# Attention and gated MLP on one core: block 0's transposes behind two QKV tiles, the projection of blocks 2 and 3 a chunk later, two ties more

## The chip, the cores and the metric

The kernel runs on one core of a Trainium2 chip. The metric is device time in microseconds (us), from start to end of one execution; lower is better. The profile is of one execution. Its engines are PE (TensorE, matmul), PEld (PE's weight loads), DVE (VectorE), ACT (ScalarE), POOL (GpSimd) and SP (SyncE, which here only issues DMAs). Each works through its own instructions in order and waits for the others by semaphores.

## The reference

One layer for 2048 tokens of width 576, in float32. First attention with 32 heads of 18 channels, in which a token sees itself and seven earlier ones at distances 2, 4, ... 14; then a gated MLP of hidden width 4608. Both add to their input, and both are preceded by a layer norm without weights.

```python
h  = x + attn(layernorm(x) @ wqkv) @ wo
g  = layernorm(h) @ w_gate
u  = layernorm(h) @ w_up
h2 = h + (sigmoid(g) * u) @ w_down
```

## The kernel before

**Blocks.** Since attention only joins tokens of equal parity, the tokens are four blocks of 512: even ones, first and second half (blocks 0 and 1), and odd ones likewise (blocks 2 and 3). A block is four tiles of 128 tokens (NS = 4).

**Precision.** Every float32 operand is split in a high and a low part by `split` (lines 103 to 105: ACT copies the high part, line 104, DVE subtracts it, line 105; `split_rest`, lines 108 and 109, for the last 64 of 576 rows). A product is three matmuls: high by high, low by high, high by low. The transposes that come before are matmuls with the identity (`tr_main`, line 139, and `tr_rest`, line 143).

**Front.** `qkv` (line 377) computes the QKV projection of a block for a quarter of the heads, one token tile of 14 matmuls (`tok_major`, lines 146 to 153) at a step, copies it out on ACT (line 384) and sends it to DRAM. `attention` (line 162) is DVE work on windows that are loaded back: products (182, 208), sums (186, 214, 216, 219) and the softmax between (194 to 200, Exp on ACT). `step(ag, n)` moves it on by n steps; so QKV tiles are put between its steps. Block 0's result is kept in `o` (a `tok` tile, line 409 completes it), that of the other blocks goes to DRAM (lines 221 and 223).

**Block 0's projection.** `front` (line 478) transposes `o`, multiplies it by the output weights, adds the input (line 255), normalises (`ln_j`, lines 113 to 135) and transposes again for the MLP. In before (lines 502 to 521) two of its steps, the transposes, come right behind block 0's attention, tied with `issue_after(last)` behind the last QKV tile emitted; its other steps stand between the QKV tiles of blocks 2 and 3 for the last quarter of heads. `issue_after(x)` keeps an instruction behind x in the order of x's engine.

**Main loop** (line 1078). It goes over 86 chunks c: 14 of kind "std" for block 0 (`single`, line 623), 22 of kind "pair" for blocks 0 and 1, 14 "std" for block 1, 36 "pair" for blocks 2 and 3. NF is 36 and NSTD 14. A chunk is 128 of the 4608 hidden channels: gate and up products (`prod`, line 588, and `rest`, line 595), a Sigmoid on ACT, a product on DVE. "Pair" handles two blocks with seven products in place of eight (`pair`, line 649), whose operands and results are sums. Its copies, sums and Sigmoids have lines 654 to 678. `load_gu` (line 544) loads the next weights `wg` on SP; `weights` (line 554) splits them. Down products (`down_tile`, line 697) are copied or added to a `stage` tile (lines 705 and 707), and POOL's DMA of line 713 adds a full one to `hacc` in DRAM.

**Background work.** At fixed places in a chunk `bg_step` takes one step of a generator: `under_first` for block 1, `under_rest` (line 882) for blocks 2 and 3: attention, then `proj_scr` (line 792) of each. `proj_scr` loads the attention output `oj` (one tile per three steps), the weights `wow` and the input `hj`, all by `load_j` and `paced` (line 549), tied behind the last weight load on SP (`behind`); transposes, multiplies and normalises them. `wos_early` (line 779) loads half of the output weights into two `tl` tiles. In `under_rest` the projection of block 2 may begin from chunk NF on (line 893). Between the blocks, line 901 clears a `stage` tile on POOL, from which ACT writes zeros to DRAM (line 903).

**Last 36 chunks.** Here the down products of blocks 2 and 3 are in sevens too (`down_seven`, line 748: matmuls 759, copies 765). Their weights `wd` come in a load of their own (`load_down`, line 972) for two chunks at a time; `down_side` (line 982) forms sums of them on DVE (lines 1003 to 1006) and splits them into `d` tiles (`pair_d`) at steps 0, 4 and 6 of an odd chunk. The seven products are queued behind `lag(LAG)`, three empty steps, in the first case (f == 1).

**Results.** Near the end of each block's accumulation in `hacc`, line 1083 copies `hacc[0]` and `hacc[1]` to the output from POOL.

The order within an engine is made by a scheduler from the order of emission and the priorities (`tc.high_priority`).

## Time and profile before

| | |
|---|---|
| median of three runs | 1597.37 us (1594.46 to 1597.83) |
| the profiled execution | 1599.5 us, of which the span from first to last instruction 1597.7 |
| mean granted PE clock | 0.996 |
| busy: PE, DVE, ACT, POOL | 1561.7, 1268.7, 874.0, 185.4 us |
| DMA | 273.50 MB, mean 171 GB/s |

In the views below a group or wait is named by engine, line and `out<-in` tiles. In a list of waits, "PE acc L143 <- DVE tok L409: 4.5, 1, 4.5" says that PE's instruction of line 143 writing `acc` stood for DVE's instruction of line 409, 4.5 us in all, once, at most 4.5. In a timeline a row has the start, the duration, engine, line, operation and tiles, "xN" for N instructions in a run, and in brackets the idle time before it and what ended it. In a chain of waits a row is start, duration and what the end of the program then hung on. PE clock is the share of full speed that was granted.

### The profile page before, as it was taken

The numbers are of one execution on the slowest core, as the hardware profiler recorded it, in microseconds if no ns is written. First come the engines' busy times: TensorE is split into PE (matmuls) and PEld (weight loads), VectorE is DVE, ScalarE is ACT, GpSimd is POOL, SyncE is SP. The second block draws the span as 40 slices with busy tenths as digits, with TensorE's granted clock in tenths as the row PEclk, the third lists the DMA queues.
The fourth block names the chain that finished last, engine by engine and source line by source line (L and its number), as shares of the span: only waits on it lengthen the run. The fifth ranks groups of instructions, "written<-read, shape, count | busy, mean of one in ns | idle before, by whom it ended". The sixth has DMA issues, their size and how long they took to land.

```text
span 1597.7 us, 22339 instructions
## 1 busy us (share of the span) xinstructions
PE 1561.7 (98%) x8532; PEld 1381.1 (86%) x8532; DVE 1268.7 (79%) x1922; ACT 874.0 (55%) x1535; POOL 185.4 (12%) x226
## 2 busy tenths in 40 slices
PE   7999899999999999999999999999999999999998
PEld 6899888898888888888898887888888888888887
DVE  7999999769999999999355777776677776677755
ACT  5432235334556555656434444766777676677761
POOL 1000010010000100000120100112112111211110
PEclk9999999999999999999999999999999999999999
DMA  7564545534566676666864225889888989888983
GB/s 268 200 210 161 193 183 195 200 115 174 133 169 163 165 178 172 166 181 146 239 207 152 84 94 141 164 172 177 169 170 188 176 166 183 172 167 179 187 171 119
DMA packets 76699, 273.50 MB, mean 171 GB/s; under 512 B 8272, under 2 KB 14160, under 8 KB 75696
## 3 DMA queue, kind: packets, MB, share of 16 engines
q0 software_dynamic: 27856, 106.47, 35.3%
q1 hardware_dynamic: 40304, 143.70, 27.4%
q10 hardware_dynamic: 8432, 21.89, 3.6%
q8 instruction: 67, 1.10, 0.3%
q14 instruction: 40, 0.33, 0.1%
HBM read 145.88 MB, written 128.52 MB: 172 GB/s over the span
## 4 chain that ended last, share of the span: by engine, by line
PE 83%; DVE 9%; DMA 5%; issue 2%; ACT 1%; SPq 0%; POOL 0%; ACTq 0%; POOLq 0%; DVEq 0%
PE b L588 41%; PE dp L697 13%; PE dp L759 11%; PE b L595 7%; PE acc L150 6%; DMA wg<-in_wmlp_dram 1%; PE b L150 1%; DVE pr L208 1%; PE bgp L150 1%; DVE tl L105 1%; DMA x<-tok 1%; DVE w L105 1%; DMA ar<-x 1%; DMA oj<-o 1%; DVE stage L707 1%
## 5 line engine op out<-in xcount | busy, mean ns | idle before, releaser
L588 PE MATMUL b<-tl,w 128*128 128x512 f32 x1728 | 443.2, 396 | 2.5 <-ACT w L104 2.2
L588 PEld LDWEIGHTS b<-tl,w 128*128 128x128 f32 x1728 | 312.0, 188 | 63.1 <-ACT w L104 3.0
L588 PE MATMUL b<-th,w 128*128 128x512 f32 x1380 | 360.2, 395 | 3.0 <-ACT s L671 1.7
L588 PEld LDWEIGHTS b<-th,w 128*128 128x128 f32 x1380 | 251.1, 188 | 57.1 <-DVE s L672 5.5
L595 PE MATMUL b<-th,w 128*128 128x512 f32 x576 | 177.7, 390 | 0.0
L104 ACT ACTIVATE w<-wg 128x384 fp32r<-128x384 f32 (+2 forms) x200 | 118.2, 596 | 103.2 <-PE b L595 40.5
L765 ACT ACTIVATE ev<-dp 128x576 f32<-128x576 f32 x224 | 145.1, 648 | 33.8 <-PE dp L759 31.0
L105 DVE TENSOR_TENSOR w<-wg,w 128x384 fp32r<-128x384 f32 (+2 forms) x200 | 128.3, 648 | 43.9 <-ACT w L104 43.6
L768 POOL DMA_DIRECT2D h<-ev x128 | 109.4, 855 | 457.1 <-ACT ev L765 445.0
L150 PE MATMUL acc<-qw,th 128*128 128x432 f32 x512 | 155.9, 365 | 1.0 <-DVE th L109 0.9
L105 DVE TENSOR_TENSOR w<-tw,w 128x512 fp32r<-128x512 f32 x116 | 79.6, 687 | 72.4 <-ACT w L104 71.4
L595 PEld LDWEIGHTS b<-th,w 128*128 128x128 f32 x576 | 108.4, 188 | 23.3
L104 ACT ACTIVATE w<-tw 128x512 fp32r<-128x512 f32 x116 | 73.2, 631 | 92.3 <-PE b L588 83.2
L697 PE MATMUL dp<-d,h1h 128*128 128x288 f32 x640 | 119.5, 296 | 2.8 <-ACT stage L705 2.8
L697 PE MATMUL dp<-d,h0h 128*128 128x288 f32 x640 | 118.5, 295 | 0.9 <-DVE tail L707 0.9
L697 PEld LDWEIGHTS dp<-d,h1h 128*128 128x128 f32 x640 | 98.6, 189 | 5.9 <-ACT stage L705 3.0
L697 PEld LDWEIGHTS dp<-d,h0h 128*128 128x128 f32 x640 | 98.9, 188 | 4.6 <-DVE tail L707 1.2
L150 PEld LDWEIGHTS acc<-qw,th 128*128 128x128 f32 x512 | 97.2, 190 | 5.8 <-DVE th L109 1.2
L150 PE MATMUL acc<-qw,tl 128*128 128x432 f32 x256 | 92.7, 362 | 0.0
L384 ACT ACTIVATE ev<-acc 128x432 f32<-128x432 f32 x64 | 33.8, 531 | 106.9 <-PE acc L153 98.3
L705 ACT ACTIVATE stage<-dp 128x576 f32<-128x576 f32 x96 | 61.9, 648 | 53.9 <-PE dp L697 42.7
L182 DVE TENSOR_TENSOR pr<-kw,q 128x2304 f32<-128x2304 f32 x32 | 81.7, 2552 | 4.4 <-DMA kw<-k 4.2
(270 smaller groups left out, 2886.3 us busy)
## 6 DMA issues: line engine op xcount, KB each, us to landing
h<-ev POOLq DMA_DIRECT2D x96, 576.0 KB, 6.8
wg<-in_wmlp_dram SPq DMA_DIRECT2D x49, 928.0 KB, 5.4
h<-stage POOLq DMA_DIRECT2D x24, 1152.0 KB, 11.1
wg<-in_wmlp_dram SPq DMA_DIRECT2D x36, 640.0 KB, 4.9
kw<-k SPq DMA_DIRECT2D x16, 792.0 KB, 4.3
vw<-v SPq DMA_DIRECT2D x16, 792.0 KB, 5.2
wd<-in_wmlp_dram SPq DMA_DIRECT2D x18, 576.0 KB, 6.6
h<-ev POOLq DMA_DIRECT2D x32, 288.0 KB, 6.1
```

What stands on the lines that cost most here:

```text
L104: act.activation(hi, src, AF.Copy)
L105: splits.append(dve.tensor_tensor(lo, src, f32(hi), ALU.subtract))
L150: pe.matmul(ps[:, :n], a[:, c, js], m[:, c], start=k == 0, stop=False)
L182: dve.tensor_tensor(pr, both(kw, u), q[:, us].unsqueeze(2).broadcast_to([P, 2, W, CG]), ALU.mult)
L384: act.activation(ev[:, :, j], ps[:, :NQ].rearrange("p (t c) -> p t c", t=3), AF.Copy)
L588: pe.matmul(ps, wt[:, a, k0 + c], xx[:, m + c], start=first and k == 0, stop=k == 5, skip_group_check=True)
L595: pe.matmul(ps, wt[:, a, k0], xx[:, 4], start=False, stop=a == 1, skip_group_check=True)
L697: pe.matmul(ps[:, i, :DH2], a[:, js], d[:, m, i * DH2:(i + 1) * DH2], start=k == 0, stop=k == n)
L705: act.activation(hv, ps, AF.Copy)
L759: pe.matmul(ps[:, i, :DH2], a[x][:, js], m[y], start=k in (0, 1, 3) and q == 0, stop=q == 2, skip_group_check=True)
L765: act.activation(hs[:, k % 2], ps[:, :, :DH2], AF.Copy)
L768: pool.dma_start(hsev[:, u, k0:k + 1], hs[:, :k + 1 - k0], accum_op=ALU.add, max_dma_last_dim=8 * D)
```

## The change

1. Two of the four QKV tiles of block 2 are emitted ahead of block 0's transposes, each with a step of attention behind it. The transposes are tied behind the second of them instead of behind block 1's last tile. The two tiles that are left follow as before.
2. In `proj_scr` for block 2 there are four steps in place of three between two `oj` loads. In `under_rest` the projection of block 2, and with it that of block 3, begins from chunk NF + 1 instead of NF.
3. The Sigmoid of `s2` in `pair` is kept in `gated`. For f == 1 what `down_side` emits is tied behind the latest such Sigmoid, which for an order within one engine means ACT's copies of the `d` splits.
4. The copies to the output on POOL are tied behind the last weight load in `behind`.

```diff
@@ -505,12 +505,16 @@
         step(ag, 1 if ready else 4)
     while not ready:
         step(ag, 1)
+    more = qkv(2, 3, T[2], w[3])
+    for _ in range(2):
+        next(more)
+        step(ag, 1)
     last = passes[-1]
     with tc.issue_after(getattr(last, "ins", last)):
         for _ in range(2):
             next(fr)
     for b in (2, 3):
-        for _ in qkv(b, 3, T[b], w[3]):
+        for _ in more if b == 2 else qkv(b, 3, T[b], w[3]):
             next(fr, END)
             step(ag, 1)
         if b == 2:
@@ -645,6 +649,7 @@
         return {t: hid}
 
     added = [None]
+    gated = [None]
 
     def pair(X, w, between, last):
         b1, b2, b3 = b_tile(0), b_tile(1), b_tile(2)
@@ -675,7 +680,7 @@
         rest(b3, X["a11"], w, "g4")
         with tc.high_priority(HC):
             added[0] = dve.tensor_tensor(s2, s2, b3, ALU.add)
-            act.activation(s2, s2, AF.Sigmoid)
+            gated[0] = act.activation(s2, s2, AF.Sigmoid)
         between(5)
         prod(b1, X["s4"], w, "b11", False)
         rest(b1, X["s4"], w, "u4")
@@ -813,9 +818,8 @@
             ins = []
             for j in range(NS):
                 ins.append([load_j(pj, b, j, 0), None])
-                yield
-                yield
-                yield
+                for _ in range(3 if b == 1 else 4):
+                    yield
             ww = pj.tile([P, 2, 5, DH2], F32R, name="wow")
             paced(f32(ww), wscr[0])
             wos[0] = ww[:, 0], ww[:, 1]
@@ -894,6 +898,8 @@
             yield ATT
         if wos[1] is None:
             wos[1] = wos_early()
+        while c < NF + 1:
+            yield
         with sb_pool("pj2", "right") as pj:
             a0 = xt.tile([P, 5, TB], F32, tag="th", bufs=3, name="ar")
             ins = yield from proj_scr(pj, 2, a0, wos, after=3)
@@ -988,7 +994,10 @@
             elif f + 1 < NF:
                 load_down(f + 1)
         t = M["wd"].rearrange("p c (h n) -> p c h n", h=2)
-        with tc.high_priority(HI):
+        with ExitStack() as way:
+            way.enter_context(tc.high_priority(HI))
+            if f == 1:
+                way.enter_context(tc.issue_after(getattr(gated[0], "ins", gated[0])))
             if f >= NF - NPL:
                 if (f % 2, i) in ((0, 4), (1, 6)):
                     M[f] = d_tile()
@@ -1080,7 +1089,8 @@
         for b, late_c in ((0, NF + NSTD - 3), (1, NF + NSTD + 5)):
             if c == late_c:
                 e, hf = BLOCKS[b]
-                pool.dma_start(ov[e, hf], hacc[b])
+                with tc.issue_after(getattr(behind[0], "ins", behind[0])):
+                    pool.dma_start(ov[e, hf], hacc[b])
```

## The prediction

> **What bounds the kernel now.** I began with the page's busy times.

> ```profile
> PE 1561.7 (98%) x8532; PEld 1381.1 (86%) x8532; DVE 1268.7 (79%) x1922; ACT 874.0 (55%) x1535; POOL 185.4 (12%) x226
> ```

> TensorE (PE) is busy 98% of the span, so a change can gain only where PE stands still or runs at a reduced clock. I looked for such places in 20 us windows and cut the three that the diff touches more finely. Columns: stretch, its length, busy time of PE, PEld, DVE, ACT and POOL (instructions), granted clock, DMA share, GB/s.

> ```profile
> core 0: us, PE busy (x) PEld busy (x) DVE busy (x) ACT busy (x) POOL busy (x), PEclk, DMA share, GB/s
> 180.00:188.00 8.00, 1.77 (x14) 1.33 (x12) 7.90 (x13) 2.10 (x5) 0.00 (x0) 0.78 1.03 374
> 188.00:192.00 4.00, 4.00 (x21) 4.00 (x20) 3.94 (x6) 0.92 (x4) 0.00 (x0) 0.58 0.67 254
> 180.00:297.00 117.00, 107.64 (x587) 95.14 (x585) 113.94 (x149) 46.00 (x84) 9.11 (x9) 0.97 0.48 173
> 791.00:796.00 5.00, 2.19 (x16) 1.95 (x15) 1.81 (x4) 3.02 (x6) 0.00 (x0) 0.95 1.05 289
> 796.00:800.00 4.00, 4.00 (x18) 3.42 (x18) 1.80 (x4) 1.31 (x3) 0.70 (x1) 0.63 0.94 374
> 971.00:977.00 6.00, 4.68 (x13) 3.43 (x14) 4.09 (x9) 0.97 (x3) 1.24 (x1) 0.72 0.67 135
> ```

> Then I asked for PE's own waits in three stretches: A, 179 to 312 us (edit 1); B, 765 to 870 us (edit 2); C, 956 to 1000 us (edit 3).

> ```profile
> PE acc L143 <- DVE tok L409: 4.5, 1, 4.5
> PE b L588 <- ACT w L104: 2.2, 1, 2.2
> PE mm L139 <- DVE tok L219: 1.7, 1, 1.7
> PE bgp L139 <- DMA oj<-o: 1.3, 1, 1.3
> ...
> PE dp L697 <- ACT stage L705: 2.8, 1, 2.8
> PE b L143 <- DVE tl L105: 0.9, 1, 0.9
> ...
> PE b L588 <- ACT s L671: 1.7, 1, 1.7
> PE b L588 <- DVE s L672: 1.0, 1, 1.0
> ```

> Stretch A holds two waits on block 0's attention output and one on the first GLU weights; B one wait on an ACT copy; C two waits on the sum that the pair forms. Each is followed by a reduced clock: 0.58 in 188 to 192, 0.63 in 796 to 800, 0.72 in 971 to 977.

> **Edit 1 (block 0's transposes).** Two QKV tiles of block 2, of 14 matmuls each, now stand on PE ahead of the transposes. The chain of waits has eleven such matmuls end to end:

> ```profile
> 219.72 2.16 PE acc L150 x11
> ```

> That is 0.196 us each, 2.75 us a tile, 5.5 us for two. They fit into the two holes (1.7 + 4.5 = 6.2 us), which shrink to less than a microsecond, and the half-rate stretch behind them (4 us x 0.42 = 1.7) would go too: 7.2 us, if PE were what sets the end here. It is not. DVE is busy 113.94 of the 117 us from 180 to 297, so at most 117 - 113.94 = 3.1 us can be won before block 1's attention ends, and behind that end stands a chain without PE:

> ```profile
> 288.01 2.47 DVE pr L208
> ...
> 296.08 4.50 DMA o<-kw
> ...
> 302.52 8.35 DMA oj<-o
> ```

> DVE makes the last products, the result goes to DRAM, comes back as `oj`, and PE waits 1.3 us for it at 311. PE time won at 184 is waited away there unless DVE is earlier as well. DVE loses no instruction by the edit. In the new order its first GLU weight's low half has the same work ahead of it:

> ```profile
> 233.14 1.29 DVE L105 TENSOR_TENSOR w<-wg,w 128x640 fp32r<-128x640 f32 x2
> ```

> Walking that order with before's durations I come to 233.05 instead of 233.14. PE ends its QKV work some 6.6 us earlier and then stands in front of the first GLU products: the hole is moved, and the slow clock with it. The tiles' ACT copies fall into ACT's idle time (46.00 busy of 117). Bounds: -3.1 (all of DVE's idle time) and +1.7 (a half-rate stretch like the one of 188 us, now before work that DVE waits for). I take 0, since the walk ends next to the row.

> **Edit 2, what it takes away.** Block 2's four `oj` loads are issued on SP ahead of a weight load; in before three of them and two `tl` loads were in flight when the weight load of 779.40 was issued. It needed 13.4 us, and ACT, which works in order, stood for it:

> ```profile
> wg<-in_wmlp_dram SPq DMA_DIRECT2D x1, 928.0 KB, 13.4
> ...
> 792.86 0.74 ACT L104 ACTIVATE w<-wg 128x640 fp32r<-128x640 f32 x1 [7.66 <-DMA wg<-in_wmlp_dram]
> ```

> The `stage` copy behind it was late and PE lost 2.8 us, then 5 x 0.05 + 4 x 0.37 = 1.7 us of clock: 4.5. In the new order the `oj` loads follow that weight load, the projection's first transposes come 90 matmuls later, and the copy has its weights in time: -4.5. Block 3's loads no longer have a weight load between them on SP: I credit the 0.9 us wait on `tl`. All queues that these loads are moved past are SP's; nobody waits for the `oj` themselves before the transposes.

> **Edit 2, what it adds.** Behind the projection of block 2, line 901 clears a `stage` buffer on POOL, and ACT issues two DMAs from it (line 903). The clearing waits until the accumulation out of that buffer has landed.

> ```profile
> 819.23 2.03 POOL L901 MEMSET stage<- 128x2304 f32 x1 [12.86 <-DMA h<-stage]
> ...
> 821.72 0.65 ACT L705 ACTIVATE stage<-dp 128x576 f32<-128x576 f32 x1 [10.60 <-PE bgp L153]
> 822.27 0.59 ACT L632 ACTIVATE s<-b 128x512 f32<-128x512 f32 x1
> ```

> ACT stood 10.6 us there. (The view names PE; but it went on when the clearing ended.) In before this cost PE nearly nothing: block 2's transposes were through and matmuls of its projection stood ready. In the new order line 903 stands on ACT ahead of a Sigmoid, a `stage` copy and the `th` split of block 2's first `oj`. PE's third `oj` transposes reuse that split's bank, so they wait.

> When does each come? PE is where the first transposes used to stand at 790.78:

> ```profile
> 790.78 0.60 PE L139 MATMUL b<-ident,oj 128*128 128x128 f32 x4
> ...
> 802.30 3.21 PE dp L697 x24
> ...
> 805.62 1.40 PE b L588 x6
> ```

> A down tile of 12 takes 1.6 us, a GLU product of 14 takes 14 x 0.23 = 3.25. Then come a down tile, a product, and the down tile that fills the buffer: 790.8 + 1.6 + 3.25 + 1.6 = 797.25, with the copy and the issue about 798.5 for the accumulation. Two more down tiles and a product bring the copy ahead of line 903 (804.4); another product brings the first transposes (807.0); these, a down tile, the second ones and seven matmuls bring the third transposes, at 807.0 + 0.45 + 1.6 + 0.45 + 1.6 = 811.1.

> ```profile
> DMA to landing us min/median/max: 9.0/11.1/14.9
> ...
> DMA to landing us min/median/max: 14.0/14.7/14.9
> ```

> The first row is all 24 accumulations of this kind, the second the three of this place, beside SP's loads. With x for the landing time, the clearing (2.03), the issue (0.4), Sigmoid (0.6), copy (0.65), `th` (0.6) and its low half on DVE (0.65 each, below) end at 798.5 + x + 4.9, so PE stands for x - 7.7.

> ```profile
> 184.93 1.29 DVE L105 TENSOR_TENSOR tl<-mm,th 128x512 fp32r<-128x512 f32 x2
> ```

> SP's 1440 KB and three `hj` loads are now in flight together with it, so I take x = 14.5, among the three of this place: 6.8 us, and 1.7 us of clock behind it (as at 188). Bounds: x = 9.0 gives 1.3 us and no slow clock. Edit 2 is -4.5 - 0.9 + 6.8 + 1.7 = +3.1, from -4.1 (x = 9.0) up to +8.7, see the rivals.

> **Edit 3 (second down weights).** In C three `d` splits stand on ACT in front of the copy of line 671, and two of their low halves on DVE in front of line 672:

> ```profile
> 968.91 1.83 ACT L104 ACTIVATE d<-wd 128x576 fp32r<-128x576 f32 x3 [1.68 <-DVE wd L1005]
> 970.64 0.58 ACT L671 ACTIVATE s<-b 128x512 f32<-128x512 f32 x1
> ...
> 971.22 1.42 DVE L105 TENSOR_TENSOR d<-wd,d 128x576 fp32r<-128x576 f32 x2
> ```

> Tied behind the pair's second Sigmoid, they leave both free. The two holes (1.7 + 1.0) and the clock (6 x 0.28 = 1.7) are 4.4 us. The splits now stand behind the Sigmoid, among the next pair's copies; what is late next is the first matmul of the seven products, which has three units of lag before it. The next pair's first copy may stand behind one `d` split (1.83 / 3 = 0.6); I charge 0.7. Edit 3 is -3.7, between -4.4 (nothing behind the splits) and +0.6 (rival 4).

> [...]

> **Edit 4 (outgoing results).** The copy to `out_dram` is tied to the issue of a load that is on SP. Built with and without this tie, the kernel has the same order on every engine: 0, to be read as a part of the change that does nothing.

> **Sum:** 0 + 3.1 - 3.7 + 0 = -0.6 on the profiled execution's 1599.5 (span 1597.7 and 1.8 around it). That execution is 2.1 above the runs' median of 1597.37, so on the median's scale I forecast 1596.8. In x: the sum is x - 15.1. What this kernel's measurement can tell from no change is about 0.2%, 3.2 us: faster needs x under 11.9, slower x over 18.3.

> **The rivals.**

> 1. *ACT's stand at line 903 stays hidden.* The accumulation lands in 9.0, since the `oj` loads no longer crowd it: PE stands 1.3 us without a slow clock, the sum is 1.3 - 5.4 - 3.7 = -7.8, time 1589.6. For it: the median of all 24 is 11.1. Against: all three of this place took 14 or more.

> 2. *The accumulation queues behind the outgoing copy* (the slower side). Both are POOL's, and the copy is issued just before:

> ```profile
> 797.32 0.70 POOL L1083 DMA_DIRECT2D out_dram<-h  x1 [13.75 <-DMA h<-stage]
> ...
> DMA to landing us min/median/max: 6.8/7.0/7.3
> ```

> In before the copy had landed (797.3 + 6.8 = 804.1) when the accumulation was issued, at 805. Now the accumulation is issued 1 us behind it. If its bytes go after the copy's, x = 804.1 - 798.5 + 14.5 = 20.1: the sum is +5.0, time 1602.4. Against: the copy waits for an accumulation that may land earlier itself, as the loads in its way are fewer.

> 3. *Edit 1 wins DVE's idle time:* -3.1 more, 1593.7. For it: PE and ACT offer DVE its inputs sooner. Against: DVE's idle time is spread over many short waits.

> 4. *Edit 3 only moves its wait:* six splits (two groups of three like the 1.83 us above) delay the next pair's copies as they delayed line 671, and one split more stands ahead: C is +0.6 instead of -3.7, the sum +3.7, time 1601.1. Against: no PE product waits for a down weight before the lag is over.

> 5. *The slow clock in B and C isn't due to the holes* and stays when they go: 1.7 + 1.7 less is gained, the sum is +2.8, time 1600.2. Against: in 791 to 796 the clock is still 0.95 and in 796 to 800, right behind the hole, 0.63; and 188 to 192 shows the same behind the longest hole. [...]

> **How the numbers follow.** Forecast 0.36, rival 1 0.27, rival 2 0.20, rival 3 0.08, rival 4 0.06, rival 5 0.03. Faster is rivals 1 and 3, 0.35; same is the forecast and rival 5, 0.39; slower is rivals 2 and 4, 0.26. The predicted time is the forecast's, 1596.8; its own range is x = 11.9 to 18.3, 1594.2 to 1600.6. The range over all reaches beyond rival 1 by half of edit 1's gain (1588) and to rival 2 with edit 1's +1.7 (1604).

> **What would show it.** Edit 1: PE busy through 180 to 192 at a clock near 1, and a hole of some 9 us before the first GLU products, near 224 to 233; `oj` still waited for at 302 to 311. Edit 2: no wait on `stage` at 791, the weight load of 779 landing before 791; the clearing of line 901 at 813, and a PE wait on `tl` or ACT of 5 to 8 us near 811. Edit 3: no wait on lines 671 and 672 near 970. The forecast is wrong if attention of block 1 ends more than 3 us earlier, if the clearing starts before 810 or after 817, or if C's holes come back within the next 30 us.

## The result and the profile after

The change makes the kernel slower by 0.2%: 1599.03 us (median of 20 runs, 1595.97 to 1602.96) against 1595.68 (20 runs, 1592.63 to 1601.00), a ratio of 1.002 with a 95% interval of 1.0011 to 1.0028, or +3.2 us (+1.8 to +4.5). In a second session the same kernel came to 1.0015 (1.0005 to 1.0025), or +2.4 us. The forecast was -0.6 us.

The two profiled executions say something else: their spans are 1597.7 us before and 1596.1 after, 1.6 less. Before's profiled execution (1599.5) lies 3.8 above the median of its 20 runs, after's (1597.87) 1.2 below that of its own. That contradiction is what most of the experiments are about.

After, in windows of the stretches that the prediction cut, with some more (columns as there: busy time of PE, PEld, DVE, ACT, POOL, granted clock, DMA share, GB/s):

```profile
180.00:188.00 8.00, 6.68 (x44) 6.16 (x43) 7.87 (x11) 3.72 (x10) 0.00 (x0) 1.00 0.99 346
188.00:192.00 4.00, 4.00 (x31) 4.00 (x32) 3.97 (x9) 0.00 (x0) 0.00 (x0) 1.00 0.52 219
...
220.00:224.00 4.00, 2.66 (x14) 2.20 (x12) 4.00 (x3) 1.78 (x3) 0.34 (x1) 1.00 0.90 303
224.00:230.00 6.00, 2.07 (x4) 1.12 (x4) 5.90 (x5) 2.83 (x6) 0.00 (x0) 0.57 1.00 415
230.00:234.00 4.00, 1.44 (x3) 1.16 (x4) 4.00 (x6) 1.31 (x2) 0.00 (x0) 0.50 0.38 141
...
791.00:796.00 5.00, 5.00 (x28) 4.39 (x27) 1.16 (x2) 1.18 (x2) 0.71 (x1) 1.00 0.54 108
796.00:800.00 4.00, 4.00 (x29) 3.83 (x29) 1.98 (x3) 3.44 (x6) 0.94 (x1) 1.00 0.82 291
...
811.00:816.00 5.00, 0.46 (x3) 0.03 (x1) 0.00 (x0) 0.00 (x0) 1.73 (x1) 0.93 1.03 396
816.00:820.00 4.00, 0.84 (x5) 0.84 (x5) 1.58 (x3) 3.05 (x6) 0.30 (x1) 0.50 0.99 393
...
971.00:977.00 6.00, 6.00 (x27) 4.71 (x27) 2.10 (x4) 2.16 (x4) 1.24 (x1) 1.00 0.64 103
```

The three holes of before are gone: PE works through 180 to 192 at full clock but for 1.3 us, and through 791 to 800 and 971 to 977 without a pause. Two new ones stand at 222 to 234 and at 811 to 820, with the clock at half behind or in them. PE's waits after:

```profile
PE b L139 <- DVE tl L105: 7.7, 1, 7.7
PE b L592 <- DVE w L105: 4.3, 1, 4.3
PE b L592 <- ACT w L104: 3.6, 1, 3.6
...
PE mm L150 <- DVE tl L105: 1.3, 1, 1.3
PE b L139 <- DMA oj<-o: 1.1, 1, 1.1
```

The first is the new hole of stretch B, the next two are in front of the first GLU products. How the first comes about stands in three timelines of after, POOL's, ACT's and PE's (start, duration, instruction, idle time before it):

```profile
795.12 0.71 POOL L1093 DMA_DIRECT2D out_dram<-h  x1 [11.07 <-DMA h<-stage]
799.07 1.20 POOL L718 DMA_DIRECT2D h<-stage  x1 [3.24 <-ACT stage L710]
814.27 2.02 POOL L907 MEMSET stage<- 128x2304 f32 x1 [14.01 <-DMA h<-stage]
```

```profile
804.84 0.64 ACT L710 ACTIVATE stage<-dp 128x576 f32<-128x576 f32 x1
816.33 0.38 ACTq L909 DMA_DIRECT2D h<-stage  x1
816.75 0.60 ACT L636 ACTIVATE s<-b 128x512 f32<-128x512 f32 x1 [11.28 <-POOL stage L907]
...
817.78 0.60 ACT L104 ACTIVATE th<-b 128x512 fp32r<-128x512 f32 x1
```

```profile
811.07 0.39 PE L592 MATMUL b<-th,w 128*128 128x512 f32 x1
819.16 1.12 PE L139 MATMUL b<-ident,oj 128*128 128x128 f32 x4 [7.71 <-DVE tl L105]
```

(Line 909 is 903 of before, 907 is 901, 592 is 588.) The accumulation is issued at 799.07 and the clearing starts at 814.27, so x was 15.2; ACT stands 11.3 us; PE arrives at the third `oj` transposes just after 811 and waits 7.7 us.

In what follows, "lost" in a place is PE's wait there plus what its matmuls took over their pitch at full clock (0.23 us for 512 columns, 0.196 for 432, 0.13 for 288), worked out from the starts of consecutive matmuls in the trace. Before's first profile lost 4.9 us at 791 to 800, 2.0 at 856 to 864 and 4.7 at 969 to 977; after's lost 9.7 at 809 to 823 and 12.0 at 222 to 239.

### The profile page after: what moved, and what is told of

Same layout as the page of the kernel before. It is cut to its first block, busy times and chain, and to the rows that moved or that the text cites. A ratio compares the mean times of both kernels' runs of the same rounds, so it can differ in the third digit from the quotient of the medians.

```text
span 1596.1 us, 22337 instructions
## 1 busy us (share of the span) xinstructions
PE 1559.3 (98%) x8532; PEld 1380.6 (87%) x8532; DVE 1269.8 (80%) x1922; ACT 872.1 (55%) x1535; POOL 182.3 (11%) x226
## 4 chain that ended last, share of the span: by engine, by line
PE 86%; DVE 8%; DMA 4%; issue 1%; ACT 1%; POOL 0%; SPq 0%; ACTq 0%; POOLq 0%; DVEq 0%
PE b L592 42%; PE dp L702 14%; PE dp L764 11%; PE b L599 8%; PE acc L150 6%; PE b L150 1%; PE bgp L150 1%; DVE pr L182 1%; DVE pr L208 1%; DMA h<-stage 1%; DVE lg L186 1%; DVE pr L214 1%; DMA ar<-x 1%; DVE tl L105 1%; PE acc L152 0%
## 5 line engine op out<-in xcount | busy, mean ns | idle before, releaser
L104 ACT ACTIVATE w<-wg 128x384 fp32r<-128x384 f32 (+2 forms) x200 | 118.1, 596 | 101.7 <-PE b L599 46.0
L150 PE MATMUL acc<-qw,th 128*128 128x432 f32 x512 | 155.4, 364 | 0.9 <-DVE th L109 0.9
L105 DVE TENSOR_TENSOR w<-wg,w 128x384 fp32r<-128x384 f32 (+2 forms) x200 | 128.4, 649 | 31.2 <-ACT w L104 31.0
L105 DVE TENSOR_TENSOR w<-tw,w 128x512 fp32r<-128x512 f32 x116 | 79.7, 688 | 70.2 <-ACT w L104 69.2
L104 ACT ACTIVATE w<-tw 128x512 fp32r<-128x512 f32 x116 | 73.3, 632 | 91.2 <-PE b L592 83.2
L150 PEld LDWEIGHTS acc<-qw,th 128*128 128x128 f32 x512 | 97.2, 190 | 5.9 <-DVE th L109 1.1
L150 PE MATMUL acc<-qw,tl 128*128 128x432 f32 x256 | 92.9, 363 | 0.0
## 6 DMA issues: line engine op xcount, KB each, us to landing
wg<-in_wmlp_dram SPq DMA_DIRECT2D x49, 928.0 KB, 5.3
h<-stage POOLq DMA_DIRECT2D x24, 1152.0 KB, 11.1
```

The source lines that it names most:

```text
L104: act.activation(hi, src, AF.Copy)
L105: splits.append(dve.tensor_tensor(lo, src, f32(hi), ALU.subtract))
L150: pe.matmul(ps[:, :n], a[:, c, js], m[:, c], start=k == 0, stop=False)
```

## The experiments

Theory 1: the two profiles are typical, and the terms can be read off them. Theory 2: before's profiled execution was untypical in the places that the change touches. All ratios are to the kernel before, run in the same session.

### The kernel before again, and each edit alone

No edit; a second profile and more times.

> The kernel before once more, for a second profile. Theory 1 (the two profiles are typical): PE loses about 4.9 us around 791 to 800 and 4.7 around 969 to 977, as in the first profile of it. Theory 2 (the profiled execution of before, 3.8 above the median of its 20 runs, was untypical in a place that the change touches): at least one of the two is smaller by 2 us or more. Its time is the same as before's within 0.2%.

Ratio 0.9991 (0.9977 to 1.0006), as it should be. Its profile lost only 2.0 us at 791 and 1.3 at 969, 6.3 us less than the first one in these two places. Theory 2.

Edit 1 alone (the first hunk of the diff).

> Edit 1 alone. Theory 1: the hole of 180 to 192 (8.6 us of PE time lost there) goes and one of about 10 to 12 us comes in front of the first GLU products; the attention of block 1 ends within 1 us of before's 294.4 to 295.2, net 0 to +1 us. Rival (PE sets the end here): 3 us or more are gained.

Ratio 0.9999 (0.9984 to 1.0014), -0.2 us (-2.6 to +2.2). It lost 1.6 us at 186 to 188 instead of 8.6 at 180 to 191, and 10.6 at 222 to 235 instead of 3.1; attention ended at 293.3 instead of 294.4. The hole is moved and nothing gained, as theory 1 had it.

Edit 2 alone (the fourth and fifth hunk).

> Edit 2 alone. Theory 1: the hole at 791 (4.9 us) and the one at 856 (2.0) go, PE stands for 7 to 8 us near 811 and loses 9 to 10 with the clock; net +2.5 to +4 us. Theory 2, with the hole at 791 usually smaller: +5 to +8 us.

Ratio 1.0031 (1.0016 to 1.0046), +4.9 us (+2.6 to +7.3), near the border of the two expectations. It lost 9.0 us from 811 to 824. This one edit costs more than the whole change.

Edit 3 alone (the second, third and sixth hunk).

> Edit 3 alone. Theory 1: the two waits near 970 are gone with nothing in their place, net -4 to -5 us. Theory 2, with these waits usually smaller in before: 0 to -2 us.

Ratio 0.9981 (0.9968 to 0.9994), -3.0 us (-5.1 to -1.0): a gain between the two expectations. Both waits near 970 are gone and no wait of PE is left from 960 to 1000. In its profile the hole at 791, which it doesn't touch, lost 4.0.

### What the profiles of the same code lose

Eight of the profiled kernels have before's order at 791, nine have it at 969 (a kernel with edit 2 alone still has the hole at 969, and so on; d0 and d1 are told of below). PE's wait (at 969 the two waits together), the lowest clock in any window of 5 us just behind it, and what was lost:

| kernel | at 791: wait, clock, lost | at 969: wait, clock, lost |
|---|---|---|
| before, first | 2.8, 0.66, 4.9 | 2.7, 0.66, 4.7 |
| before, second (b0) | 1.6, 1.00, 2.0 | 1.1, 1.00, 1.3 |
| before, third (b1) | 2.7, 0.66, 4.8 | 1.6, 0.66, 3.6 |
| edit 1 (e1) | 2.8, 0.66, 5.0 | 1.8, 0.66, 3.9 |
| edit 3 (e3) | 1.9, 0.66, 4.0 | - |
| edits 1 and 3 (e13) | 1.9, 1.00, 2.2 | - |
| edit 2 (e2) | - | 2.2, 0.66, 4.1 |
| halves of edit 2 (e2a, e2b) | - | 1.8, 1.00, 2.3; 1.2, 1.00, 1.8 |
| before with less on DVE (d0) | 2.1, 1.00, 2.5 | 1.5, 1.00, 2.0 |
| edit 1 with less on DVE (d1) | 2.6, 1.00, 2.9 | 1.7, 1.00, 2.2 |
| mean | 3.5 lost | 2.9 lost |

The third profile of before was a run for this question:

> The kernel before a third time, for a third profile. Theory 2 (the waits at 791 and 969 are short, and only some executions lose clock behind them): each place loses either 1 to 2.5 us at full clock or 3.5 to 5 us at reduced clock. Theory 1: both lose the 4.9 and 4.7 of the first profile.

It lost 4.8 and 3.6, the upper case in both places. The three profiles' spans go with these losses: 1597.7 and 1596.9 us with both, 1591.4 with neither. Over all the profiles the two cases of theory 2 are there. The same wait loses clock in one execution and not in another. Edit 3 alone, PE's wait and the window of the 5 us behind it:

```profile
PE dp L698 <- ACT stage L706: 1.9, 1, 1.9
```

```profile
795.00:800.00 5.00, 5.00 (x24) 4.43 (x23) 2.76 (x5) 2.21 (x5) 0.71 (x1) 0.66 1.01 391
```

Edits 1 and 3, the same two views:

```profile
PE dp L702 <- ACT stage L710: 1.9, 1, 1.9
```

```profile
795.00:800.00 5.00, 5.00 (x31) 4.31 (x30) 2.18 (x4) 2.54 (x6) 0.70 (x1) 1.00 0.92 363
```

Both waited 1.9 us, and one got a clock of 0.66 behind it (24 matmuls in 5 us), the other 1.00 (31 matmuls). Of 17 such waits between 1.1 and 2.8 us, 8 lost clock, about 2 us each time beside the wait, with waits from 1.6 to 2.8; nine didn't, with waits up to 2.6.

How the cases differ can be followed in the traces. In the profiles of before and after the granted clock is either 1.00 or 0.50, and all its changes lie whole multiples of 3.4133 us apart, to within 4 ns over the whole run. (In before it is 0.50 from 184.56 to 191.38, from 795.54 to 798.96 and from 973.04 to 976.45; the second and third of these start 179 and 179 + 52 such lengths after the first.) Such a length is called a step here. From 18 us on, seven steps at full clock in these two profiles were followed by a slow one: PE was busy in them for 0.66, 1.35, 0.97 and, at the very end, 0.00 of 3.41 us in before, and for 1.24, 0.00 and, near the end, 1.48 in after. In every other step at full clock it was busy for 1.59 us or more (the least is before's at 228.93). A slow step costs a busy PE 1.7 us (half of 3.413) and makes 0.66 of a window of 5 us. So the author's reading is that a short wait loses clock when enough of it falls into one step; no run tests that by itself. Here are two waits of nearly the same length, in windows cut at the steps. In before's third profile the wait of 2.7 us at 791 lies in one step, PE is busy for 0.71 of its 3.41 us, and the next step is slow:

```profile
792.34:795.75 3.41, 0.71 (x6) 0.47 (x5) 0.83 (x1) 1.73 (x4) 0.00 (x0) 1.00 1.08 265
795.75:799.17 3.42, 3.42 (x16) 3.40 (x16) 2.09 (x4) 1.94 (x6) 0.70 (x1) 0.50 1.02 399
```

In edit 1 with less on DVE the wait of 2.6 us is divided between two steps, with 2.30 and 1.93 us of PE, and the clock stays:

```profile
787.41:790.82 3.41, 2.30 (x13) 1.70 (x11) 0.00 (x0) 0.00 (x0) 0.00 (x0) 1.00 1.05 262
790.82:794.24 3.42, 1.93 (x15) 1.93 (x16) 1.93 (x4) 3.06 (x7) 0.00 (x0) 1.00 1.08 318
794.24:797.65 3.41, 3.41 (x20) 2.85 (x19) 2.23 (x4) 1.70 (x3) 0.70 (x1) 1.00 0.99 392
```

### The changed kernel again

> The changed kernel once more, for a second profile. Theory 1: PE's wait near 811 is 7 to 8 us again and 9 to 10 are lost there with the clock, since the gap is always longer than what the clock forgives. Rival (its wait varies as before's waits do): less than 6 or more than 12 us lost. Its time is 1599 within 0.2%.

Ratio 1.0015, median 1597.29. PE's wait on `tl` was 7.8 us, and 10.8 were lost: as theory 1 said, if a little over its 10. The new hole is there each time and costs clock in all three profiles that have it in this form (7.7, 7.8 and, with edit 2 alone, 7.0 us), unlike the two that it replaces. A wait longer than two steps of 3.413 us holds a whole one wherever it starts: in after's first profile that is the step from 811.93 to 815.34, with PE busy for 0.00 us of it, and the clock is 0.50 from 815.34 to 822.17.

### The writes of zeros issued by POOL

```diff
-                act.dma_start(hsev[:, u, 1:6:2],
+                pool.dma_start(hsev[:, u, 1:6:2],
```

> The changed kernel, but the two writes of zeros (line 909 there, 903 in before) are issued by POOL behind its own clearing, so ACT does not stand for it. Theory 1 (ACT's stand costs the 9.7 us lost from 809 to 823): it gains 8 to 10 us on the changed kernel, about 1590, and no PE wait over 1 us is left from 805 to 830. Rival (the stand goes to another engine, or the transfers are what is late): less than 3 us are gained and PE stands for `hj` or `stage` in the same place.

Ratio 0.9999 (0.9988 to 1.0010): 3.4 us better than the changed kernel's 1.002 in the first session, 2.6 better than its 1.0015 in the second, each with some 2 us either way. That is clearly not the 8 to 10 of theory 1; whether it is under the rival's 3 can't be told. ACT no longer stands for POOL. It stands for a weight load instead; ACT's and PE's timeline of this kernel:

```profile
812.87 0.74 ACT L104 ACTIVATE w<-wg 128x640 fp32r<-128x640 f32 x1 [6.40 <-DMA wg<-in_wmlp_dram]
```

```profile
815.41 1.11 PE L139 MATMUL bgp<-ident,oj 128*128 128x128 f32 x4 [3.92 <-DVE tl L105]
```

PE's wait is 3.9 us instead of 7.7, one transposition later, and 6.9 are lost in place of 9.7. ACT stood 6.40 us for that weight load, up to 812.87, while the accumulation of 797.05 was in flight: POOL waited 13.79 us for its landing, up to 812.04. So the hole has, as these rows read, two causes one behind the other: ACT's wait at line 909, and behind it the transfers that edit 2 has moved here from 771 to 797, with a wait for a weight load like the one that ACT had there (7.66 us, up to 792.86).

### The two halves of edit 2

Four steps between the `oj` loads, but from chunk NF on:

> Edit 2 without its second half: four steps between the `oj` loads of block 2, but the projection still from chunk NF on. Theory 1 (the later chunk brings line 903's wait under PE's path): the hole at 791 is smaller or gone, ACT's stand falls where PE has matmuls left, -3 to 0 us against before. Rival (the spacing brings it): +3 us or more.

The projection a chunk later, but three steps between the loads:

> The second half of edit 2 alone: the projection a chunk later, three steps between the `oj` loads. Theory 1: PE stands behind line 903 as with both halves, +3 to +6 us against before. Rival: 0 to -3 us, the hole at 791 gone and nothing in its place.

Ratios 1.0055 (1.0037 to 1.0074) and 1.0048 (1.0032 to 1.0065): +8.8 and +7.7 us. By these numbers each is worse than both together (+4.9, +2.6 to +7.3), though the intervals overlap and the sessions differ. Theory 1 missed the first half, where the rival held: the spacing alone brings PE under line 903's wait too (on `th`), and it keeps some of the hole at 791 besides. For the second half it had the wait, and the cost came out above its 3 to 6. PE's timeline with the first half:

```profile
818.48 0.48 PE L143 MATMUL bgp<-ident,oj 128*128 128x128 f32 x1 [7.71 <-DVE th L109]
```

And with the second:

```profile
809.95 0.63 PE L139 MATMUL bgp<-ident,oj 128*128 128x128 f32 x4 [1.91 <-DMA oj<-o]
...
819.11 0.48 PE L143 MATMUL b<-ident,oj 128*128 128x128 f32 x1 [5.72 <-DVE tl L105]
```

The second half loses `oj` time ahead of the same wait, since three `oj` loads in a row are again ahead of a weight load. Delaying this projection by either means lands it on the wait that before passed without harm.

### Edits 1 and 3 without edit 2

> Edits 1 and 3 without edit 2. If the edits add up as their single runs say (0.0, -2.0): about 1593.5, and 5 to 6 us under the changed kernel. Rival (edits 1 and 3 hinder each other): no better than edit 1 alone, 1596.

Median 1592.28, ratio 0.9977 (0.9965 to 0.9988), -3.7 us (-5.6 to -1.9): faster than both kernels. The single runs of edits 1 and 3 add up to -3.2, so it bears out that these two parts add up, and that edit 2 is the one to leave out.

### What sets the end of stretch A

```diff
-            dve.tensor_tensor(pr[:, :, 0:4], pr[:, :, 0:4], pr[:, :, 4:8], ALU.add)
+            dve.tensor_tensor(pr[:, :, 0:2 if b == 1 and g else 4],
+                              pr[:, :, 0:2 if b == 1 and g else 4],
+                              pr[:, :, 4:6 if b == 1 and g else 8], ALU.add)
```

On the kernel before, and on edit 1 alone:

> The kernel before with six of DVE's additions of line 214 (block 1's last three quarters of the heads) at half their width, so half of those additions is left out: about 6 x 0.65 = 3.9 us less of DVE work between 182 and 295 us. Theory 1 (DVE sets the end of this stretch): 3 to 4 us are gained. Rival (PE sets it): within 1 us of before.

> Edit 1 with the same six additions at half their width. Theory 1: it gains as much on edit 1 alone (1596) as d0 on before, 3 to 4 us, so edit 1 stays worth nothing. Rival (PE sets the end once DVE is relieved): edit 1 gains 3 us or more over d0.

d0 is 0.9994 (0.9982 to 1.0006), -1.0 us (-2.9 to +1.0), and d1 0.9999 (0.9987 to 1.0011), -0.2 us. The expected 3 to 4 us did not come; the rival of d1 failed as well, for edit 1 wins nothing when DVE has less to do. In d0 PE's waits on `oj` at 302 to 311 are gone, as they should be if DVE was late there, and attention ends at 292.1, 2.3 us earlier (in d1 at 292.3, only 1.0 earlier than with edit 1); but those waits were only 2.0 us in before's first profile, so PE has no more to win there, and the hole in front of the GLU lost 5.8 in d0 against 3.1 (4.1 in the second and third profiles of before). That would fit DVE and PE both being within some 2 us of setting the end, but these runs don't show it: the interval of d0 reaches from nothing to -2.9 us, and the scheduler also puts some instructions around the shortened ones in another order, on PE too, so that this is not a clean removal.

## Why the prediction was wrong

The steps against what was measured, in us; the last column is the edit run alone (in the sum, the whole change), the traces' column the mean of the lost times of all profiles that have the place.

| step | forecast | by the traces | by the times of the runs |
|---|---|---|---|
| edit 1 | 0 | hole moved | -0.2 (-2.6 to +2.2) |
| edit 2: hole at 791 | -4.5 | -3.5 | |
| edit 2: block 3's `oj` | -0.9 | -1.9, and 1.0 of small new waits later | |
| edit 2: the stand at line 903 | 6.8 + 1.7 | +9.8 | |
| edit 2 | +3.1 | +5.4 | +4.9 (+2.6 to +7.3) |
| edit 3 | -3.7 | -3.2 (2.9 at 969, 0.3 at 981) | -3.0 (-5.1 to -1.0) |
| sum | -0.6 | about +2 | +3.2 (+1.8 to +4.5) |

**What held.** Each mechanism is in the trace where the prediction put it. Edit 1 moved its hole and won nothing. The hole at 791 went. ACT's stand at line 903 came under PE's path: PE reached the third transposes at 811, x was 15.2 for the 14.5 taken, and PE waited 7.7 us for the 6.8. Edit 3 removed both waits and put none in their place; the 0.7 charged for a split ahead of a copy did not show. Edit 4 has no run of its own; with edit 2 alone, without it, the copy to the output also stands right ahead of the accumulation on POOL (797.48 and 800.67). Of the rivals, 1 fell (x was nowhere near 9), 3 fell (edit 1 alone, -0.2 us, with -3.1 outside its interval) and 4 fell; 2, the accumulation behind the outgoing copy, fell too, though that copy did go out first: it was issued at 795.12, and x stayed at 15.2.

**What failed: the size of the gains.** The step was "5 x 0.05 + 4 x 0.37 = 1.7 us of clock: 4.5" at 791, and "the two holes (1.7 + 1.0) and the clock (6 x 0.28 = 1.7) are 4.4" at 969. Both were read off one execution, in which both waits were at the long end and both had lost clock. The 1.7 us of clock is right for one slow step (half of 3.413), but of 17 waits this short only eight brought one. Over eight and nine profiles the first hole is worth 3.5 and the second 2.9. So 8.9 us of expected gain were 6.4. That is 2.5 of the 2.8 us between the forecast's -0.6 and the +2.2 that the traces add up to; the other differences, 1.3 more for the new hole (below) against the 0.7 that edit 3 was charged in vain and 0.3 that it gained at 981, nearly cancel. The profiled execution of before stood 2.1 above the three runs shown and, as it turned out, 3.8 above the median of 20; the prediction took that off as a constant from both sides of the comparison. It was not a constant: it was to a good part these two holes, the ones that the change removes.

**A second, smaller size.** The new hole was put at 6.8 + 1.7 and measured 9.7, 10.8 and 9.0 in three profiles (9.8 on the mean). PE's wait was 7.0 to 7.8 us for the 6.8, and the slow clock cost 2 to 3 us rather than 1.7, since more than one step was slow (in the first profile two, from 815.34 to 822.17; in the second the clock was 0.65 over 811 to 816 and 0.50 over 816 to 820). Unlike the old holes, this one had a slow clock behind or in it in all three.

The sum by the traces is edit 2's +5.4, edit 3's -3.2 and nothing for edit 1: about +2, inside the interval of the first session (from +1.8) and of the second (+0.8 to +4.0). What is left is within what the runs can tell.

**Rival 5**, that the slow clock isn't due to the holes, is not borne out in that form: where the waits went, the clock stood at 1.00 (after, 791 to 800 and 971 to 977). But the prediction took the rows of one profile as typical. Over 17 waits of 1.1 to 2.8 us the truth lies between: nine cost no clock and eight did. What the length leaves open goes, in the steps shown above, with PE's busy time in them: 0.71 of 3.41 us ahead of a slow step, 2.30 and 1.93 ahead of full ones.

**Stretch A** was right in its result and only half right in its reason. The bound by DVE's idle time, 3.1 us, holds in that edit 1 wins nothing; but that DVE alone sets the end did not come out in d0, where six additions of 1.35 us took 0.75, 3.6 us less in all, and 1.0 us was gained (at most 2.9). After's timeline of ACT has another wait in the moved hole:

```profile
231.13 0.74 ACT L104 ACTIVATE w<-wg 128x640 fp32r<-128x640 f32 x1 [1.23 <-DMA wg<-in_wmlp_dram]
```

That is the second chunk's weight load. How the new hole is shared between it, ACT's order and DVE was not taken apart further.

## What to carry to other kernels

Before a hole is priced, look at it in several executions: here eight of 17 waits of 1.1 to 2.8 us were about 2 us dearer by the clock, and the distance of before's profiled execution from the median (3.8 us) was a hint that it had two of them. Price a removed hole by its mean and a new one by the mean too; here a short hole (3.5 us lost on the mean) was traded for a long one (9.8), which cost time even though the pair of profiles showed 1.6 us won. And when work is moved later to avoid one queue of transfers, look for the in-order wait that it is moved onto (here a DMA issue on ACT that waits for a clearing on POOL, 11.3 us in after), because what was free in the old place was free only by position.
